# Turning q and k by whole 64-token transposes instead of 64 x 64 products, with loads cut by head

## The chip, the cores and the metric

The kernel runs on one core of one Trainium2 chip. The core has a matrix engine (TensorE, "PE" in the profile, with its weight loads shown apart as "PEld"), a vector engine (DVE), a scalar engine (ACT), GpSimd (POOL) and SyncE (SP), which issues most of the DMAs. The engines run side by side and wait for each other through semaphores. The metric is the device time in microseconds (us) of one execution.

## The reference, cut to what matters

Inputs are q, k and v of shape (8 batches, 8 heads, 576 tokens, 64), a number tau, and the weights of one feed-forward layer.

```python
scores = (1 / 8) * q @ k.T                                # per batch and head, 576 x 576
thresh = scores.max(-1) - tau
attn   = softmax(where(scores >= thresh, scores, -1e9))
x      = (attn @ v) with the heads side by side           # 4608 tokens x 512
h      = x @ w_in                                         # 4608 x 1024
solu   = h * softmax(h)
out    = layernorm(solu) * g_ln @ w_out                   # 4608 x 512, float32
```

## The kernel before

Tokens of a head are split into 512 "main" tokens, laid as 128 partitions times 4 tokens, and 64 "end" tokens. Work on the scores is cut into 144 slots (18 per batch), and the main loop is a loop over rounds, one slot per round. The order of the work on every engine is written out by hand in that loop; no scheduler changes it.

TensorE is used in quarters: nearly all of its products have 64 rows and 64 columns, so that four of them, one per quarter of the array, run side by side. The profile shows this form as `64*64`. A float32 product appears there as two weight loads and two matmuls. In one round TensorE does, in its own order: turns of q and k for a later batch, where some are due (L282); the scores of a slot (L412); one half of the first layer for 128 tokens (`ff_h`, L572) or of the second (`ff_o`, L676); and the product of the attention weights with v for a pair of slots (`attend_steps`, L516). In the last rounds, when no slot is left, the first layer is done by products over the whole array instead (L562, shown as `128*128`).

The scores need q and k with the head dimension on the partitions, so both are turned on TensorE. A pair is two heads of one batch; there are 4 pairs per batch and 32 in all. For a pair, `q_item` and `k_item` turn four blocks (one for each of the 4 tokens of a partition) and `e_item` one block with the end tokens. A block is made by `turn` (L276): for the lower and the upper 64 partitions (r) and the two heads of the pair (y), one 64 x 64 product with a piece of the identity, whose result lands in a spare part of the PSUM tiles that the scores of the round use. So a pair takes 9 calls of `turn`, 36 products. Batch 0 has its own path: its pairs are turned at the start (L767, L822) and by `whole_pair` (L367) in rounds 0, 2 and 4. Pairs of batches 1 to 7 are in the list `preps` (L722), each with the round from which it is due; in a round, as many items as fit into seven spare blocks are turned just ahead of the scores. ACT and DVE copy the turned blocks out (`keep`, L315, L319, L340, L356, L360).

q and k come in by `load_one` (L120), for half a batch (four heads) at a time: one DMA of 512 KB from the SP queue, of 128 partitions x 4 heads x 4 tokens x 64 numbers, so 512 runs of 1 KB. For the first half of a batch it also loads the end tokens of all eight heads (`load_ends`, L138): 64 partitions x 8 heads x 64 numbers, 512 runs of 256 bytes. Rounds for the loads are in `load_at` (L736).

The other DMAs of the SP queue are, in every pair of rounds, four that reorder the transposed attention weights (`blocks`, wT<-T, L491), four that swap halves of a normalised layer (`ff_swap`, V<-u, L654), two stores (L703), and loads of v (L159, L164). SP works through its queue in order. The DMAs are counted on eight semaphores in turn, so each issue also waits until the DMA eight places ahead of it has landed.

## Time and profile before

| | us |
|---|---|
| median of 4 executions | 899.48 (896.93 to 901.35) |
| the profiled execution | 901.35 |
| its span, first to last instruction | 899.4 |
| PE busy | 846.9 (94%) |
| DVE busy | 679.8 (76%) |
| ACT busy | 590.3 (66%) |
| POOL busy | 451.0 (50%) |

A line of a group reads: source line, engine, operation, tiles written and read, form and shape, count; then busy time and the mean duration of one in ns; then the idle time just before, and what ended it. Matmuls overlap, so the mean duration of one is its latency and not the time after which the next can begin; that one is read from starts in the timeline, where a row holds the start, the time from the first start to the last end, and how many instructions are merged.

### The profile page before, as it was taken

Reading aid. Unit: us, or ns where it says so; the run is one execution under the profiler, and the core shown is the slowest. Engines: PE = TensorE matmul, PEld = TensorE weight load, DVE = VectorE, ACT = ScalarE, POOL = GpSimd, SP = SyncE. Lnnn points to the kernel's source line nnn. Section 1 sums busy time; section 2 is a strip of 40 time slices with the busy share of each in tenths; the row PEclk is TensorE's granted clock in tenths of the full one; section 3 lists DMA queues with packets and bytes.
Section 4 is the critical chain, followed back from the end, with each engine's and each line's share of the span. In section 5 each row is a group of like instructions: output and inputs, shape, how many; then the busy total and the mean of one; then the engine's idle time right before and its main releaser. Section 6 shows DMA issues by size and latency. Waiting matters only on the chain. (4 is left out here: it accounts for less than half of the span.)

```text
span 899.4 us, 39683 instructions
## 1 busy us (share of the span) xinstructions
PE 846.9 (94%) x17089; PEld 654.3 (73%) x17089; DVE 679.8 (76%) x1312; ACT 590.3 (66%) x1241; POOL 451.0 (50%) x871
## 2 busy tenths in 40 slices
PE   4668899999999989999999999999999999999997
PEld 3445577878688767777788887878788777777655
DVE  5999886888777757777777877777877877787352
ACT  5867776777777756677766766677767766666121
POOL 2556555555455554555555555555555555555120
PEclk9788899999999999999999999999999999999999
DMA  7999879796867785877886777877887756756322
GB/s 235 247 231 270 215 182 206 176 220 152 216 163 168 165 182 120 187 169 161 192 182 174 179 162 175 187 177 160 186 185 181 180 129 137 171 138 137 78 48 48
DMA packets 95502, 154.61 MB, mean 172 GB/s; under 512 B 27224, under 2 KB 69216, under 8 KB 95328
## 3 DMA queue, kind: packets, MB, share of 16 engines
q1 hardware_dynamic: 94192, 150.09, 71.7%
q8 instruction: 134, 2.20, 1.1%
q10 hardware_dynamic: 1136, 2.00, 0.7%
q14 instruction: 40, 0.33, 0.1%
HBM read 46.14 MB, written 9.44 MB: 62 GB/s over the span
## 5 line engine op out<-in xcount | busy, mean ns | idle before, releaser
L434 DVE CUSTOM_DVE_ANT_0 w<-s_ps,tau_t 128x576 f32<-128x576 f32 x280 | 200.7, 754 | 134.8 <-PE s_ps L412 112.1
L449 ACT ACTIVATE w<-s_ps,nth 128x576 f32<-128x576 f32 x280 | 201.7, 744 | 119.7 <-DVE nth L434 99.2
L676 PE MATMUL o_ps<-w,uT 64*64 64x256 f32 x4608 | 269.7, 376 | 2.0 <-issue 1.0
L676 PEld LDWEIGHTS o_ps<-w,uT 64*64 64x64 f32 x4608 | 234.5, 133 | 44.0 <-issue 10.9
L468 POOL TENSOR_SCALAR w<-w,sm 128x576 f32<-128x576 f32 x288 | 218.1, 769 | 14.3
L572 PE MATMUL h_ps<-w,xh 64*64 64x512 f32 x1856 | 222.1, 591 | 0.9 <-issue 0.9
L458 ACT ACTIVATE w<-w,ntau 128x576 f32<-128x576 f32 x288 | 220.5, 773 | 0.0
L480 DVE STREAM_TRANSPOSE T<-w 128x576 f32<-128x576 f32 x288 | 205.8, 751 | 6.4 <-POOL w L468 6.1
L516 PEld LDWEIGHTS pv<-wT,v 64*64 64x64 f32 x5760 | 171.1, 136 | 38.7 <-issue 22.5
L412 PE MATMUL s_ps<-kT,qT 64*64 64x512 f32 (+1 forms) x2048 | 175.9, 425 | 17.3 <-ACT w L449 16.3
L516 PE MATMUL pv<-wT,v 64*64 64x128 f32 (+1 forms) x5760 | 173.2, 264 | 9.4 <-issue 6.5
L572 PEld LDWEIGHTS h_ps<-w,xh 64*64 64x64 f32 x1856 | 118.0, 134 | 81.3 <-issue 54.1
L465 POOL TENSOR_SCALAR sm<-sm 128x2 f32<-128x2 f32 x144 | 36.4, 253 | 264.8 <-ACT w L458 261.9
L466 POOL TENSOR_TENSOR sm<-sm,mone 128x2 f32<-128x2 f32 x144 | 105.3, 731 | 12.0
L412 PEld LDWEIGHTS s_ps<-kT,qT 64*64 64x64 f32 x2048 | 69.5, 140 | 25.8 <-ACT w L449 21.1
L638 ACT ACTIVATE V<-u,nb,rs 128x1024 f32<-128x1024 f32 x36 | 44.7, 1241 | 52.6 <-POOL nb L628 52.6
L539 ACT COPY xh<-pv 128x256 f32<-128x256 f32 x64 | 23.7, 370 | 62.8 <-PE pv L516 62.8
L587 DVE TENSOR_REDUCE hm<-h_ps 128x1 f32<-128x1024 f32 x36 | 43.1, 1196 | 22.1 <-PE h_ps L572 16.5
L458 ACT ACTIVATION_READ_ACCUMULATOR w<-w,ntau 128x1 f32 x288 | 57.2, 199 | 0.0
L596 ACT ACTIVATE u<-h_ps,hm 128x1024 f32<-128x1024 f32 x36 | 40.3, 1118 | 20.7 <-DVE hm L587 10.3
L602 DVE TENSOR_TENSOR u<-h_ps,u 128x1024 f32<-128x1024 f32 x36 | 42.8, 1190 | 10.4 <-ACT u L596 10.4
L664 DVE STREAM_TRANSPOSE uT<-V 128x1024 f32<-128x1024 f32 x36 | 43.8, 1217 | 9.1 <-DMA V<-u 9.0
(81 smaller groups left out, 632.7 us busy)
## 6 DMA issues: line engine op xcount, KB each, us to landing
wT<-T SPq DMA_DIRECT2D x288, 288.0 KB, 5.7
V<-u SPq DMA_DIRECT2D x144, 64.0 KB, 3.6
out_dram<-ob SPq DMA_DIRECT2D x71, 128.0 KB, 2.8
v<-in_v_dram SPq DMA_DIRECT2D x16, 512.0 KB, 6.3
v<-in_v_dram SPq DMA_DIRECT2D x32, 256.0 KB, 5.8
q<-in_q_dram SPq DMA_DIRECT2D x15, 512.0 KB, 6.2
k<-in_k_dram SPq DMA_DIRECT2D x15, 512.0 KB, 5.7
raw<-in_moe_w_out_dram SPq DMA_DIRECT2D x8, 512.0 KB, 7.5
```

The lines of the kernel that those rows point to most:

```text
L412: nc.tensor.matmul(out=ps[h][ROWS[y], ks], lhsT=lhsT, rhs=d["kT"][ROWS[h], ks], start=True, stop=True,)
L434: nc.vector.tensor_tensor_reduce(out=w, in0=ps[:, 0:S], in1=(zero if loose else tau_t).to_broadcast([P, S]), scale=1.0, scalar=BIG, op0=AL ...
L449: nc.scalar.activation(out=d["w"][x], in_=d["w"][x] if d["loose"] else d["ps"][x][:, 0:S], func=AF.Prelu, bias=d["nth"][x], scale=-1.0, al ...
L458: nc.scalar.activation(out=w, in_=w, func=AF.Exp, bias=ntau, scale=1.0, accum_out=sm[:, x : x + 1])
L466: nc.gpsimd.tensor_tensor(out=sm, in0=sm, in1=mone, op=ALU.pow)
L468: nc.gpsimd.tensor_scalar(out=w, in0=w, scalar1=sm[:, x : x + 1], scalar2=1.0, op0=ALU.mult, op1=ALU.mult)
L480: nc.vector.transpose(out=T[:, :, r, h, :], in_=w)
L516: nc.tensor.matmul(out=to, lhsT=d["v"][ROWS[u], h0 + h, m ^ 4 * u if m < 8 else m], rhs=rhs, start=m == 0, stop=m == NK - 1,)
L572: mm = nc.tensor.matmul(out=h[ROWS[y], f], lhsT=x[ROWS[r], c, ROWS[y]], rhs=w1_parts[ROWS[r], c, part ^ r], start=part == 0 and c == 0, st ...
L638: nc.scalar.activation(out=V, in_=u, func=AF.Identity, bias=nb, scale=rs)
L664: nc.vector.transpose(out=uT, in_=d["V"].rearrange("p y (m x) -> p m y x", x=32))
L676: nc.tensor.matmul(out=d["o"][ROWS[z], 512 * r : 512 * r + 256], lhsT=d["uT"][ROWS[r], m].rearrange("p y x -> p (y x)"), rhs=w2[ROWS[r], m ...
```

## The change

For batches 1 to 7 a block is turned by two transposes of 64 partitions x 128 numbers (64 tokens of both heads of the pair at once), where it was turned by four 64 x 64 products. The two heads of a pair must then lie side by side in one row of the loaded tile. So the tile is laid out as (head pair, token, 2 x 64), and `load_one` fills it by four DMAs, one per head, each of 128 partitions x 4 tokens in runs of 256 bytes. The end tokens already lie side by side. Batch 0 is turned and loaded as before. On PE the order of the items is the same as before, with half as many products in each turn; on SP each q or k load of batches 1 to 7 stands as four DMAs in the place of one; the order on DVE, ACT and POOL is unchanged.

```diff
@@ load_one
+        if b > 0:
+            d[nm] = loads.tile([P, 2, 4, 2 * D], F32, tag=nm, name=nm)
+            for x in range(4):
+                nc.sync.dma_start(
+                    out=d[nm][:, x // 2, :, D * (x % 2) : D * (x % 2) + D],
+                    in_=src[b, 4 * hf + x, 0:SM, :].rearrange("(p t) d -> p t d", t=4),
+                )
+            if hf == 0:
+                if b not in ends:
+                    ends[b] = loads.tile([P, H, D], F32, tag="ends", name="ends")
+                load_ends(b, nm, slice(0, H), nc.sync)
+            return
         d[nm] = loads.tile([P, 4, 4, D], F32, tag=nm, name=nm)
@@ turn
-    def turn(spare, x, lhsT_of):
+    def turn(spare, x, of, whole):
         o = spare["base"] + 64 * x
         to = slice(o, o + 64)
         for r in range(2):
+            if whole:
+                nc.tensor.transpose(
+                    out=spare[r][:, to], in_=of[ROWS[r]], identity=ident[ROWS[r], ROWS[r]]
+                )
+                continue
             for y in range(2):
                 nc.tensor.matmul(
-                    out=spare[r][ROWS[y], to], lhsT=lhsT_of(r, y), rhs=ident[ROWS[r], ROWS[r]],
-                    start=True, stop=True,
-                )
+                    out=spare[r][ROWS[y], to], lhsT=of[ROWS[r], y],
+                    rhs=ident[ROWS[r], ROWS[r]], start=True, stop=True,
+                )
+
+    def tokens_of(i, nm, t):
+        src, h0 = source(i)
+        if i < NP:
+            return src[nm][:, h0 : h0 + 2, t]
+        return src[nm][:, h0 // 2, t]
@@ q_item (k_item the same with "k"), e_item
-                turn(spare, x + t, lambda r, y: src["q"][ROWS[r], h0 + y, ts.start + t])
+                turn(spare, x + t, tokens_of(i, "q", ts.start + t), i >= NP)
...
-            turn(spare, x, lambda r, y: ends[i // NP][ROWS[r], 2 * (i % NP) + y])
+            two = ends[i // NP][:, 2 * (i % NP) : 2 * (i % NP) + 2]
+            turn(spare, x, two.rearrange("p y d -> p (y d)") if i >= NP else two, i >= NP)
```

## The prediction

> **What bounds the kernel now.** First the page: PE 94% busy, and in its row of 40 slices nine tenths or more from the sixth on, but for one. Then the windows by stage.

> ```profile
> span 899.4 us, 39683 instructions
> PE 846.9 (94%) x17089; PEld 654.3 (73%) x17089; DVE 679.8 (76%) x1312; ACT 590.3 (66%) x1241; POOL 451.0 (50%) x871
> ...
> 400.00:500.00 100.00, 100.00 (x2106) 81.41 (x2102) 78.18 (x151) 69.43 (x146) 54.13 (x105) 1.00 0.77 179
> 500.00:600.00 100.00, 98.77 (x2114) 82.42 (x2110) 77.65 (x152) 69.44 (x147) 53.18 (x108) 1.00 0.75 172
> ```

> After the span come PE, PEld, DVE, ACT, POOL, the granted clock and the DMA share. From about 100 us on PE is the bound, at full clock; DVE has a fifth of its time free, the DMA engines a quarter. Busy time alone can hide slack, so I read starts in PE's timeline.

> ```profile
> 505.95 0.28 PE L282 MATMUL s_ps<-ident,k 64*64 64x64 f32 x4
> ...
> 506.65 0.22 PE L412 MATMUL s_ps<-kT,qT 64*64 64x64 f32 x1
> ...
> 507.62 3.77 PE L572 MATMUL h_ps<-w,xh 64*64 64x512 f32 x32
> 511.06 2.19 PE L516 MATMUL pv<-wT,v 64*64 64x128 f32 x70
> 513.02 0.22 PE L412 MATMUL s_ps<-kT,qe 64*64 64x64 f32 x1
> ```

> The 32 passes of L572 take 3.44 us from start to start of what follows: four quarters side by side, no hole. The 24 products of a turn block (48 passes) take 505.95 to 506.65, 0.70 us, 29 ns a product. So a microsecond added to PE here lengthens the run by nearly one, and one saved shortens it.

> **What goes.** 28 pairs x 9 turns x 4 = 1008 products (L282 on s_ps: 896 + 896 + 224 rows, two passes each). At 29 to 31 ns, as the blocks after 200 us show them, 30.2 us.

> **What comes.** 28 x 9 x 2 = 504 transposes. The trace has one transpose, of the gains:

> ```profile
> L190 PE MATMUL g_ps<-ident,g_rows 8*128 8x8 f32 x1 | 0.2, 222 | 1.2 <-ACT qe L356 1.2
> L190 PEld LDWEIGHTS g_ps<-ident,g_rows 8*128 8x128 f32 x1 | 0.1, 133 | 2.5 <-ACT qe L356 2.5
> L562 PEld LDWEIGHTS h_ps<-w,xh 128*128 128x128 f32 x48 | 8.8, 190 | 11.1 <-issue 10.3 <-DVE T L480 0.8
> L282 PEld LDWEIGHTS s_ps<-ident,k 64*64 64x64 f32 x896 | 24.8, 137 | 5.6 <-ACT w L449 4.2 <-DVE both L434 0.5 <-issue 0.3
> ```

> It is one pass, not two, and its load of 128 columns takes 133 ns, like a product's load of 64 columns (median 135) and not like one of 128 (190). In L282's rows a quarter starts a new pass every 60 ns, with that 64-column load hidden behind the pass before. I take 60 ns for a transpose in one half of the array; the two halves (r = 0, 1) hold different rows and run side by side, as the quarters do: 30 ns each, 504 x 30 = 15.1 us. Bounds: 15 ns, a pass's share now (7.6 us); and, if the halves take turns, 60 ns (30.2 us). In series without any overlap, 222 ns each, it would be 112 us; no row here runs so. I stay at 30, since the load's duration is the nearest row.

> [...]

> **Changes of form.** Today turns, scores, layers and pv are all `64*64` and join without a hole. The transposes are 64 rows x 128 columns. They stand in 49 separate blocks on PE (21 of 10 transposes, 14 of 8, 7 of 14, 7 of 12), so PE goes into another form and back 49 times. The trace shows such changes at the end, into `128*128`:

> ```profile
> 823.43 3.70 PE L562 MATMUL h_ps<-w,xh 128*128 128x512 f32 x8
> 827.06 2.20 PE L516 MATMUL pv<-wT,v 64*64 64x128 f32 x72
> 829.18 3.70 PE L562 MATMUL h_ps<-w,xh 128*128 128x512 f32 x8
> 832.82 0.89 PE L516 MATMUL pv<-wT,v 64*64 64x128 f32 x24
> ```

> The same half layer takes 823.43 to 827.06, 3.63, where L572 took 3.44: 0.19 more. The pv block takes 2.12 (827.06 to 829.18) where 511.06 to 513.02 was 1.96: 0.16 more. Together 0.35 us for one change there and back: PE waits about 0.09 each time until the array is empty, and the first weight load is not hidden. With a first load as short as 64 columns it is 0.30; with quarters that end less evenly before a turn, 0.35. I take 0.33: 49 x 0.33 = 16.2 us. Bounds: 0, if only a change of the row split empties the array (the rows stay halved here), and 0.5 (24.5 us).

> [...]

> PE waits ahead of some blocks anyway (idle before L282 on s_ps: 3.5 + 6.3 + 0.5 us, on ACT and DVE); entries there are free: -1.5 us.

> **Loads.** Each of the 28 loads of q or k becomes four DMAs: 84 more on SP, the same bytes.

> ```profile
> L129 SPq DMA_DIRECT2D q<-in_q_dram x17: 392/600/1716, 0.7 to 681.8; - x17
> L140 SPq DMA_DIRECT2D ends<-in_q_dram x9: 612/690/2230, 1.2 to 631.9; - x9
> SPq L491 <- DVE T L480: 196.6, 51, 11.4
> PEld pv L516 <- DMA wT<-T: 1.8, 4, 0.9
> ```

> An issue with 512 runs of 256 bytes takes 0.69 us (the end tokens do it today), so a load takes SP 2.8 us instead of 0.6, about 60 us in all. Queued behind are the wT, V and store DMAs. SP has the time: it waits 196.6 us for the transposed T just ahead of the wT issues that mostly follow a load, and wT lands a median 4 us ahead of its pv (landings against PE's starts). Behind a load SP's wait is 0.1 to 7 us; after 425, 539 and 631 us it is only 0.1, but there wT lands 3 to 6 us early. In the stage of 60 to 110 us four loads meet waits of 1.3, 1.2, 4.1 and 1.0 us and wT is hardly early; I charge 1 us. Between 0, if all is covered, and 28 x 2.2 = 62 us, if nothing were. The packets: 256-byte ones took a mean 21.9 ns in the trace's packet records, 1 KB ones 64.8, so 28 x 512 x (4 x 21.9 - 64.8) = 327 us over 16 engines, 20 us each, 2.3 points of DMA share above 0.75. Hidden behind PE; without that cover it shows in the wT waits above. Where q or k itself is concerned: loads are due 3 to 6 rounds (over 18 us) ahead of their turn, so nothing waits for their later landing.

> The copies on ACT and DVE, their order and their sizes stay: 0.

> **Sum.** -30.2 + 15.1 + 16.2 - 1.5 + 1 = +0.6 us on the profiled execution of 901.35 (span 899.4, 1.95 around it), so 902.0. That execution stands 1.9 above the median 899.48; on the median's scale 900.1. I say 900.

> **Rivals.** [...] (2) No emptying between two forms with the same row split: -16 us, 884. For: the trace shows only changes of rows and columns together. (3) Transposes at a pass's share of 15 ns: -7.5, 892. (4) SP: ten of the 28 loads push a wT 0.8 us past its pv: +8, 908. For: a fifth of the wT land under 1.5 us ahead. Against: those mostly do not follow a load. (5) The change does what it says but PE was not the limit: then nothing but the loads' cost is seen, 900 to 902; the block starts above speak against it.

> **How the numbers follow.** My forecast 0.40 (its own range 893 to 907, from 0.25 to 0.45 us a change of form), (1) 0.20, (2) 0.15, (4) 0.13, (3) 0.08, others, slower, 0.04. Half a per cent (4.5 us) is about what can be told from no change. Faster: (2) mostly, (3), a little of the forecast, 0.25. Slower: (1), (4), the forecast's upper part and the rest, 0.43. Same: 0.32. Range: 887 leaves out most of (2), 917 holds (1) with a longer change; about 2 in 10 outside.

> [...]

## The result, and the profile after

The changed kernel takes 902.76 us (median of 53 executions, 898.06 to 910.05), the kernel before 899.58 (79 executions): a ratio of 1.0043, 95% interval 1.0031 to 1.0055, so 3.9 us slower. The forecast was 900.0, in a range of 887 to 917. The two profiled executions do not show the difference: they took 901.30 and 901.35 us.

The page of the changed kernel, first its span and busy times, then the DMA queues with packets, MB and share of the 16 engines' time:

```profile
span 899.2 us, 36750 instructions
PE 847.5 (94%) x15577; PEld 527.0 (59%) x15577; DVE 679.4 (76%) x1312; ACT 590.9 (66%) x1241; POOL 451.0 (50%) x871
...
q1 hardware_dynamic: 138544, 150.10, 74.0%
q8 instruction: 122, 2.00, 1.0%
```

PE has 1512 records fewer in each column and the same busy time. The DMA share of q1 was 71.7% before; it rose by the 2.3 points that the prediction worked out.

The groups of the transposes, by form, and PE's timeline at the same work as in the prediction (there, 24 products from 505.95 to 506.65):

```profile
L294 PE MATMUL s_ps<-ident,k 64*128 64x64 f32 x224 | 15.4, 238 | 3.6 <-ACT w L470 2.9 <-DVE both L455 0.7
L294 PEld LDWEIGHTS s_ps<-ident,k 64*128 64x128 f32 x224 | 10.5, 140 | 14.3 <-ACT w L479 6.2 <-ACT w L470 4.1 <-issue 2.0
```

```profile
500.32 3.63 PE L697 MATMUL o_ps<-w,uT 64*64 64x256 f32 x64
503.77 1.16 PE L433 MATMUL s_ps<-kT,qT 64*64 64x64 f32 x16
504.75 3.63 PE L697 MATMUL o_ps<-w,uT 64*64 64x256 f32 x64
508.31 0.28 PE L294 MATMUL s_ps<-ident,k 64*128 64x64 f32 x2
508.42 0.23 PE L294 MATMUL s_ps<-ident,ends 64*128 64x64 f32 x2
508.49 0.41 PE L294 MATMUL s_ps<-ident,q 64*128 64x64 f32 x8
508.83 1.21 PE L433 MATMUL s_ps<-kT,qT 64*64 64x64 f32 x16
509.86 3.61 PE L593 MATMUL h_ps<-w,xh 64*64 64x512 f32 x32
```

The form is `64*128`, one row a transpose, loads of 140 ns. The half layer ahead of the block takes 504.75 to 508.31, 3.56 us, where the same one without a block behind it takes 3.45 (500.32 to 503.77): 0.11 for the way into the other form. The 12 transposes take 0.52. The scores behind them take 1.03, where they take 0.98 elsewhere: 0.05. Together 0.68 us, against 0.70 for the 24 products before. So where PE is the bound, turning costs what it did.

What is lost has to be looked for at another place. In the list of waits of the changed kernel, two lines stand out; the columns are the sum in us, the number and the longest:

```profile
PE pv L537 <- DMA wT<-T: 4.6, 4, 2.2
PE o_ps L697 <- DMA w<-w: 2.8, 1, 2.8
```

The first was shorter in the kernel before:

```profile
PE pv L516 <- DMA wT<-T: 1.5, 3, 0.7
```

It is no mark of the loads, though: with the turns alone changed, whose run follows below, it is 4.0 us. The second is new: the kernel before has no wait of PE for `w<-w`. These are the copies that swap the halves of the second layer's weights (`weight_d`, L269 before, L281 after), done once, while batch 1 is loaded. The first use of that layer in PE's timeline, before and after:

```profile
111.19 3.68 PE L676 MATMUL o_ps<-w,uT 64*64 64x256 f32 x62
...
115.62 3.68 PE L676 MATMUL o_ps<-w,uT 64*64 64x256 f32 x62
```

```profile
111.62 3.69 PE L697 MATMUL o_ps<-w,uT 64*64 64x256 f32 x64 [0.30 <-DVE uT L685]
...
116.08 3.22 PE L697 MATMUL o_ps<-w,uT 64*64 64x256 f32 x52
122.12 1.08 PE L697 MATMUL o_ps<-w,uT 64*64 64x256 f32 x12 [2.83 <-DMA w<-w]
```

Before, both blocks run through (the rows of 62 leave out two passes that are interleaved with other work). After, in the second one, PE stands 2.83 us with 12 of 64 passes left, until the last copy lands. SP's timeline shows why it lands late (start, time, how many issues):

```profile
104.07 0.58 SPq L129 DMA_DIRECT2D q<-in_q_dram  x1
...
106.83 3.85 SPq L491 DMA_DIRECT2D wT<-T  x4
110.72 2.16 SPq L269 DMA_DIRECT2D w<-w  x2
```

```profile
63.41 2.71 SPq L127 DMA_DIRECT2D k<-in_k_dram  x4
...
78.53 2.67 SPq L127 DMA_DIRECT2D q<-in_q_dram  x4
...
93.18 2.97 SPq L127 DMA_DIRECT2D k<-in_k_dram  x4
...
108.76 2.65 SPq L127 DMA_DIRECT2D q<-in_q_dram  x4
111.45 1.27 SPq L281 DMA_DIRECT2D w<-w  x2
112.83 3.84 SPq L512 DMA_DIRECT2D wT<-T  x4
116.72 2.25 SPq L281 DMA_DIRECT2D w<-w  x2
```

The last two copies are issued from 110.72 before and from 116.72 after: the four loads of batch 1, each 2.7 to 3.0 us on SP instead of 0.4 to 0.6, stand ahead of them, and SP has almost no gap there. The DMA engines have little room either, as the windows of 60 to 116 us show, the kernel before first (the last three columns are the granted clock, the DMA share and GB/s):

```profile
60.00:116.00 56.00, 44.58 (x804) 30.04 (x800) 51.72 (x100) 39.53 (x87) 30.43 (x46) 0.88 0.96 240
```

```profile
60.00:116.00 56.00, 43.51 (x686) 26.71 (x682) 49.66 (x94) 37.84 (x85) 29.52 (x45) 0.88 0.95 211
```

The share is nearly full in both, and with the loads in 256-byte packets the stage moves 211 GB/s where 240 went before. From these four loads alone, 8192 packets of about 22 ns in place of 2048 of about 59, each of the 16 DMA engines gets 3.7 us more work in a stage where its share is 0.95 and more.

### The profile page after: what moved, and what is told of

It is laid out like the page before. It is cut to its first block, busy times and chain, and to the rows that moved or that the text cites. A ratio compares the mean times of both kernels' runs of the same rounds, so it can differ in the third digit from the quotient of the medians.

```text
span 899.2 us, 36750 instructions
## 1 busy us (share of the span) xinstructions
PE 847.5 (94%) x15577; PEld 527.0 (59%) x15577; DVE 679.4 (76%) x1312; ACT 590.9 (66%) x1241; POOL 451.0 (50%) x871
## 5 line engine op out<-in xcount | busy, mean ns | idle before, releaser
L697 PE MATMUL o_ps<-w,uT 64*64 64x256 f32 x4608 | 263.5, 376 | 4.1 <-DMA w<-w 2.8
L697 PEld LDWEIGHTS o_ps<-w,uT 64*64 64x64 f32 x4608 | 188.2, 133 | 93.4 <-issue 22.0
L593 PE MATMUL h_ps<-w,xh 64*64 64x512 f32 x1856 | 215.2, 592 | 2.6 <-issue 2.6
L537 PEld LDWEIGHTS pv<-wT,v 64*64 64x64 f32 x5760 | 157.4, 137 | 51.0 <-issue 38.1
L433 PE MATMUL s_ps<-kT,qT 64*64 64x64 f32 (+1 forms) x2048 | 166.1, 429 | 13.5 <-ACT w L470 12.4
L537 PE MATMUL pv<-wT,v 64*64 64x128 f32 (+1 forms) x5760 | 164.9, 264 | 9.1 <-DMA wT<-T 4.6
L593 PEld LDWEIGHTS h_ps<-w,xh 64*64 64x64 f32 x1856 | 76.0, 134 | 125.0 <-issue 113.3
L433 PEld LDWEIGHTS s_ps<-kT,qT 64*64 64x64 f32 x2048 | 54.8, 138 | 28.9 <-ACT w L470 17.8
L617 ACT ACTIVATE u<-h_ps,hm 128x1024 f32<-128x1024 f32 x36 | 40.2, 1117 | 21.9 <-DVE hm L608 14.6
```

The lines of the kernel that those rows point to most:

```text
L433: nc.tensor.matmul(out=ps[h][ROWS[y], ks], lhsT=lhsT, rhs=d["kT"][ROWS[h], ks], start=True, stop=True,)
L537: nc.tensor.matmul(out=to, lhsT=d["v"][ROWS[u], h0 + h, m ^ 4 * u if m < 8 else m], rhs=rhs, start=m == 0, stop=m == NK - 1,)
L593: mm = nc.tensor.matmul(out=h[ROWS[y], f], lhsT=x[ROWS[r], c, ROWS[y]], rhs=w1_parts[ROWS[r], c, part ^ r], start=part == 0 and c == 0, st ...
L697: nc.tensor.matmul(out=d["o"][ROWS[z], 512 * r : 512 * r + 256], lhsT=d["uT"][ROWS[r], m].rearrange("p y x -> p (y x)"), rhs=w2[ROWS[r], m ...
```

## The experiments

All ratios are to the kernel before on the same chip, with 95% intervals.

### The loads or the turns

First the changed kernel again, then each part alone, then a load on the turns.

> The changed kernel once more, on the chip of the next three: 1.004 times the kernel before, as already measured (1.0043), so about +4 us. It is the mark against which the two halves of the change are read.

Measured: 905.98 us, 1.0079 (1.0051 to 1.0106). PE waits 3.3 us for `w<-w` in its profile. So the ratio of one and the same kernel differs by 0.4% between two measurements; a difference of that size between runs on different chips says little.

The loads alone: turned by products of the tile laid out by pairs.

```diff
-        return src[nm][:, h0 // 2, t]
+        return src[nm][:, h0 // 2, t].rearrange("p (y d) -> p y d", y=2)
-                turn(spare, x + t, tokens_of(i, "q", ts.start + t), i >= NP)
+                turn(spare, x + t, tokens_of(i, "q", ts.start + t), False)
...                                              # k_item and e_item alike
```

> Loads of q and k by four DMAs of single heads, turns by products as before. Theory P (what is paid lies on PE, in the 49 changes of form): 0 to +1 us. Theory L (the changes of form are paid for by the shorter blocks, and what is left over comes from 84 more issues on SP and 43,000 more packets): +3 to +5 us, with the waits of pv and of the layers for DMAs as large as in the changed kernel, some 5 us and more.

Measured: 901.35 us, 1.0038 (1.0015 to 1.0060); a wait of 4.0 us for `w<-w`.

The turns alone: whole loads as before, the transposes take 128 neighbouring numbers of the tile.

```diff
-        if b > 0:
-            ...                                    # the four DMAs by head
-        return src[nm][:, h0 // 2, t]
+        at = D * (4 * h0 + t)
+        return src[nm].rearrange("p h t d -> p (h t d)")[:, at : at + 2 * D]
```

> Turns by transposes, q and k loaded by one DMA as before. Part of the computation is changed: a transpose takes 128 numbers side by side of the loaded row, which here are two neighbouring tokens of one head and not the two heads of one token, so the scores of batches 1 to 7 are of other numbers; every size, order and wait is that of the changed kernel. Theory P: +3 to +5 us. Theory L: -1 to +1 us. If both parts cost, 1 to 3 us here.

Measured: 898.84 us, 1.0003 (0.9979 to 1.0027). Nothing waits for `w<-w`; in its PE timeline the block runs through:

```profile
113.98 3.63 PE L686 MATMUL o_ps<-w,uT 64*64 64x256 f32 x64
117.55 0.47 PE L282 MATMUL s_ps<-ident,k 64*128 64x64 f32 x8
```

This and the changed kernel have the same work in the same order on PE; they differ in the loads alone, by 0.4% (by 0.76% with the repeated run, on the same chip). So the loads cost 3.5 to 7 us and the turns between -2 and +2.4.

Each transpose issued three times:

```diff
-                nc.tensor.transpose(out=spare[r][:, to], ...)
+                for _ in range(3):
+                    nc.tensor.transpose(out=spare[r][:, to], ...)
```

> The changed kernel with every transpose issued three times in a row, so 1008 more in the same 49 blocks. At 30 ns each, two halves side by side (the forecast): +30 us against the changed kernel. At 60 ns (halves in turn): +60. At 15 ns: +15. The copies of one block follow each other in the same half here, so if the load of a half can't overlap its own pass, it shows as up to 80 us.

Measured: 925.05 us, 1.0293 (1.0251 to 1.0335), 19 us more than the changed kernel on the same chip and 22 more than its median. In its PE timeline, 42 transposes stand where 14 did:

```profile
506.71 0.97 PE L295 MATMUL s_ps<-ident,q 64*128 64x64 f32 x24
507.51 0.73 PE L295 MATMUL s_ps<-ident,k 64*128 64x64 f32 x18
508.17 1.21 PE L434 MATMUL s_ps<-kT,qT 64*64 64x64 f32 x16
```

24 of them take 0.80 us, 33 ns each, and a block of 42 takes 0.565 us longer than one of 24, 31.4 ns for each one more. So the 31 to 32 ns a transpose (62 to 63 between two starts in one half of the array) holds for long blocks too. The 1008 more are 32 us of PE time, of which the run grew by about two thirds; where the rest went is told below, in the section on the prediction.

### More issues or smaller packets, and at which batch

The kernel before with its loads of batches 1 to 7 in four DMAs of 1 KB runs:

```diff
-            queue.dma_start(out=d[nm][:, part]..., in_=src[b, hs, 0:SM, :][part]...)
+            for h in [slice(i, i + 1) for i in range(4)] if b > 0 else [part]:
+                queue.dma_start(out=d[nm][:, h]..., in_=src[b, hs, 0:SM, :][h]...)
```

> Kernel before with each q and k load of batches 1 to 7 issued as four DMAs of one head, still in runs of 1 KB: 84 more issues on SP, no more data packets. Theory I (SP's issue time is what the loads cost): +3 to +4 us, most of it between 60 and 116 us of the span, where SP has no free time; the wT issues there come 3 to 6 us later. Theory D (the 256-byte packets crowd the DMA engines): 0 to +0.5 us.

Measured: 895.19 us, 0.9962 (0.9932 to 0.9993). More issues alone cost nothing, and that although PE waits for `w<-w` here too:

```profile
119.37 0.93 PE L677 MATMUL o_ps<-w,uT 64*64 64x256 f32 x10 [2.64 <-DMA w<-w]
```

The kernel before with two DMAs a load, in runs of 256 bytes:

```diff
+        if b > 0:
+            to = d[nm].rearrange("p h t d -> p (h t) d").rearrange("p (n x) d -> p x n d", x=2)
+            of = src[b, hs].rearrange("h s d -> (h s d)")[0 : P * 16 * D]
+            of = of.rearrange("(x p n d) -> x p n d", x=2, p=P, d=D)
+            for x in range(2):
+                nc.sync.dma_start(out=to[:, x], in_=of[x])
+            ...                                    # the end tokens as before
```

> Kernel before with each q and k load of batches 1 to 7 as two DMAs of 1024 runs of 256 bytes: the packets of the changed kernel with 28 more issues, not 84. Part of the computation is changed: the numbers loaded are of the right size and count, but lie in another order, so the scores of batches 1 to 7 are of other numbers. Theory I: +1 us if an issue costs the same however many runs it has, and up to +3 if its time goes with the runs. Theory D: +3 to +4 us.

Measured: 903.82 us, 1.0060 (1.0026 to 1.0094), with a wait of 2.6 us for `w<-w`. The smaller packets cost, not the number of issues: batch 1's loads take SP 1.3 to 2.1 us each here, and 1.8 to 2.8 us in the run before this one, which lost nothing. (The two loads of batch 1's end tokens, just behind them, take 2.5 and 4.0 us here and 0.6 and 0.7 us there.)

The changed kernel with batch 1 loaded and turned as before (three more conditions changed alike):

```diff
-        if b > 0:
+        if b > 1:
-        if i < NP:
+        if i < 2 * NP:
```

> The changed kernel with batch 1 loaded and turned as before, batches 2 to 7 as changed. Theory S (the loads cost where SP and the DMA engines are full, in the first 116 us, and nothing later): -2 to 0 us against the kernel before, since the blocks on PE are shorter and nothing is paid. If the cost is spread over all 28 loads: +2 to +4 us.

Measured: 893.49 us, 0.9933 (0.9909 to 0.9957). No wait for `w<-w`.

The kernel before with only batch 1's four loads cut by head (products as before):

```diff
+        if b == 1:
+            ...                                    # the four DMAs by head
```

> Kernel before with only the four q and k loads of batch 1 cut into four DMAs of 256-byte runs, turns by products. Theory S: +2 to +4 us, all between 60 and 116 us. If the cost is spread over all 28 loads: 0 to +0.6 us.

Measured: 906.58 us, 1.0082 (1.0053 to 1.0110). In its PE timeline:

```profile
115.75 3.22 PE L697 MATMUL o_ps<-w,uT 64*64 64x256 f32 x52
123.29 1.55 PE L697 MATMUL o_ps<-w,uT 64*64 64x256 f32 x10 [4.32 <-DMA w<-w]
```

and its windows around the stop (the number behind POOL's count is the granted clock):

```profile
120.90:124.30 3.40, 1.01 (x12) 0.65 (x16) 0.00 (x0) 1.24 (x1) 2.43 (x5) 0.50 0.77 213
124.30:127.70 3.40, 3.40 (x66) 2.56 (x62) 0.00 (x0) 0.58 (x1) 0.00 (x0) 0.50 1.14 236
127.70:131.10 3.40, 3.19 (x138) 3.02 (x133) 2.96 (x10) 1.37 (x5) 0.00 (x0) 0.99 0.98 227
```

Four loads of 28 are enough for the whole loss. PE stops after the same 52 passes, for 4.32 us, and works at half its clock until 127.7.

### The same again, and a kernel that is faster than both

> The changed kernel with batch 1 loaded and turned as before, once more: 0.993 times the kernel before (-6 us), as measured the first time. If that was chance: 0.996 to 1.000.

Measured, the kernel of 0.9933 once more: 893.36 us, 0.9945 (0.9925 to 0.9965).

Products throughout, loads cut by head from batch 2 on (`if b > 1`, `turn(..., False)`):

> Kernel before with the q and k loads of batches 2 to 7 cut into four DMAs of 256-byte runs, those of batch 1 whole, turns by products. Tells what the gain of the version above is made of. If it is the shorter blocks on PE: 0 to +1 us here. If it comes from cutting the loads (as the run with four 1 KB issues a load suggests): -3 to -5 us here.

Measured: 899.98 us, 1.0010 (0.9979 to 1.0041). The other 24 loads cost nothing that can be told from zero, so the place of the loads decides.

The kernel from batch 2 on, with batch 1's loads as four DMAs of 1 KB runs (both edits above):

> The version from batch 2 on, with batch 1's q and k loads issued as four DMAs of one head in runs of 1 KB, turned by products. If four issues of 1 KB help by themselves in the full stage: another -1 to -3 us, 0.990 to 0.992. If that gain belonged to the later batches: 0.993, the same as without it.

Measured: 892.02 us, 0.9923 (0.9893 to 0.9953), not to be told from the one without that edit. PE waits for `w<-w` in its trace as well:

```profile
119.56 1.07 PE L698 MATMUL o_ps<-w,uT 64*64 64x256 f32 x10 [2.85 <-DMA w<-w]
```

So this wait alone is not the loss: two kernels have it and lose nothing. When does the loss arise? The starts of the 65th transpose `T<-w` on DVE, the same work in every kernel, tell it. It starts at 200.1 us in the trace of the kernel before, at 197.4 to 200.3 us in the five others with batch 1's loads whole (mean of all six 198.9), at 199.1 and 199.6 us in the two with four 1 KB DMAs, and at 200.2 to 205.3 us in the five with 256-byte runs (mean 202.8). The means are 3.9 us apart, where the medians gave 3.5 to 7 us for the loads. So the loss arises in the first 200 us, while batch 1 is loaded and soon after. How much of it is the wait for the last copy, and how much arises ahead of it, these traces do not tell.

These two kernels, from batch 2 on and with batch 1 in four, beat the kernel before by 5 to 7 us and the changed one by 9 or more. By the blocks on PE, though, turning batches 2 to 7 saves nothing, and the turns alone gave 1.0003. PE's stops that no semaphore explains led to the last run: the same kernel with 64 transposes of the identity at the very start.

```diff
         first = dict(enumerate(tiles), base=0)
+        for _ in range(32):
+            for r in range(2):
+                nc.tensor.transpose(
+                    out=tiles[r][:, 0:64], in_=ident[ROWS[r]], identity=ident[ROWS[r], ROWS[r]]
+                )
```

> The kernel that keeps batch 1 as it was and turns batches 2 to 7 by transposes (0.9933 and 0.9945 of the kernel before), with 64 transposes of the identity (128 PE instructions with their weight loads) at the very start, where PE has nothing to do from 1.4 us until the first k lands at 5.6 us. So nothing is added to the path; every later PE instruction stands 128 places further on in PE's program. Theory A (PE's stops without a semaphore belong to the supply of its program in pieces of 256 instructions): the stops stay at places 193 beyond a multiple of 256, and so stand at other work than in the kernel without the 64, and the time may move by several us either way (0.990 to 1.002). Theory B (the stops belong to the work, or the gain has nothing to do with them): the stops stay at the same work, now 65 beyond a multiple of 256, and the time is as without the 64, 0.992 to 0.996 of the kernel before.

Measured: 900.82 us, 1.0027 (1.0007 to 1.0046). PE's timeline without the 64, then with them:

```profile
5.60 1.13 PE L299 MATMUL tp<-ident,k 64*64 64x64 f32 x32 [5.60 <-DMA k<-in_k_dram]
...
448.69 2.17 PE L697 MATMUL o_ps<-w,uT 64*64 64x256 f32 x36 [1.62 <-issue]
```

```profile
1.37 3.68 PE L790 MATMUL tp<-ident 64*128 64x64 f32 x64 [1.37 <-POOL ident masks.py:199]
5.58 1.13 PE L299 MATMUL tp<-ident,k 64*64 64x64 f32 x32 [0.52 <-DMA k<-in_k_dram]
...
244.30 1.30 PE L697 MATMUL o_ps<-w,uT 64*64 64x256 f32 x18 [0.94 <-issue]
...
537.99 0.65 PE L433 MATMUL s_ps<-kT,qT 64*64 64x512 f32 x3 [0.98 <-issue]
```

The 64 are over before the first k lands at 5.58, as it did at 5.60, and the first maximum on DVE starts at 10.3 us in place of 10.4: nothing is added to the path. Yet the median is 7 us longer, and the intervals lie apart. The stops have moved to other work. Counted in PE's recorded instructions (matmuls, weight loads and semaphore instructions), all stops after 200 us of at least 0.25 us without a semaphore stand here:

| kernel | counts at the stops | us each |
|---|---|---|
| before | 7617, 8129, 12225, 20929, 29633 | 0.46, 0.61, 3.80, 1.23, 0.91 |
| changed | 7105, 10945, 15041 | 1.67, 0.52, 2.56 |
| turns alone | 10945, 15041, 18881 | 2.02, 2.54, 1.25 |
| from batch 2 | 15809, 27073 | 1.62, 1.01 |
| from batch 2, 64 places on | 8129, 19393, 23489 | 0.94, 0.98, 0.26 |

Every one is 193 past a multiple of 256, and so are the 33 in the other nine traces. So they belong to the place in PE's program and not to the work (theory A). That these stops are what makes the 7 us is argued, not shown: the profiled execution of the last kernel was the fastest of its twelve (896.28 us), with stops of 2.2 us in all, and no trace of a slower one is there. The granted clock, on record for every execution, points the same way: its mean is 0.971 over the twelve of the last kernel, and 0.977 over the 22 without the 64 as well as for the kernel before on the last one's chip. By an estimate, 0.006 of 900 us is 5.4 us of full clock, most of the 7. One rival is untested: the last kernel ran on another chip than the two runs without the 64, which were not repeated there. The step from 0.9933 and 0.9945 to 1.0027 is twice the 0.4% by which the changed kernel's own ratio differed. So the gain of 0.6% from batch 2 on can't be put down to the turning: with the same work, moved to another place in PE's program, it was gone.

## Why the prediction was right or wrong

**What goes.** Right: 24 products in 0.70 us before, about 30 us in all.

**What comes.** Right: 31 to 32 ns a transpose where 30 was forecast (two more in a block make it 63 ns longer). The halves run side by side: a transpose started every 31 to 32 ns, with a load latency of 140. So the bound of 60 ns, for halves that take turns, falls, and with it what the chances count as (1). Rival (3), 15 ns, falls too.

**Changes of form.** Right, a little high. From the end of the last pass ahead of it to the first score, a block of 8, 10, 12 or 14 transposes takes 0.49, 0.55, 0.61 or 0.67 us where no wait falls into it, so the 49 take 27.3 us; the slower scores behind them, 49 x 0.05, make it 29.8. Without 504 transposes of 31.5 ns that leaves 0.28 a change there and back, in place of 0.33. In 45 of the 49 entries the first transpose starts 200, 306 or 520 ns after the start of the last pass, which has 128, 256 or 512 columns: 107 ns for every 128 columns, and 93 ns more each time. (The other four stand behind longer waits.) The rows stay halved, so rival (2) falls: with a change of columns alone these 93 ns are there. That they are the time until the array is empty, as the prediction has it, was its author's estimate; no trace shows what PE does in them. Against 30.2 before, PE's side is about zero (forecast with the entries behind waits: -0.4). The turns alone, at 1.0003, say the same.

**A microsecond on PE is a microsecond of the run.** True where PE does not wait, by the run with three transposes for one. Its lag behind the changed kernel, read from the starts of the transposes `T<-w` in the two profiles, grows by 13.4 us between 462 and 778 us, where the added transposes are 13.8 us of PE time. Over the whole run 32 us more on PE gave 19 to 22 us. The profiles, 25 us apart, put what is missing in two places. By 228 us the lag is 5.4 us for 8.6 us of added transposes, since in the first batches PE has waits for other engines (busy for 70.0 of the 90 us from 45 to 135 in the changed kernel), and added work goes into them. And at 442 us the changed kernel has a stop of 2.56 us with a halved clock behind it (0.5 from 445.4 to 448.8 us), which the other one does not have; there the lag falls by 4.5 us.

**Loads.** This is the term that was mis-sized: "I charge 1 us" for the stage of 60 to 110 us. With the same work on PE, the loads cost 3.5 to 7 us, and batch 1's alone gave 1.0082. The stage was the right one, and a load took SP 2.7 to 3.0 us, where 2.8 was forecast. But the wait that is new there is not one for a wT of the main loop, as rival (4) had it. It is the one for the last copy of the second layer's weights, issued 6 us later, with PE waiting 2.6 to 4.3 us in the five traces with 256-byte loads of batch 1 and, in three of them, a halved clock after it (0.50 in the windows shown above). That this wait is the whole of the cost is not shown: with four 1 KB DMAs a load PE waited 2.6 and 2.9 us at the same place, and nothing was lost. I looked behind the loads for wT alone, and I took the packets' 20 us a DMA engine at the share of the whole run, 0.75, where this stage has 0.96. For batches 2 to 7 the step held: 1.0010 with their loads cut, and SP's wait for T fell from 196.6 us to:

```profile
SPq L512 <- DVE T L501: 128.9, 39, 8.6
```

That is 68 us shorter, near the 60 us that the prediction reckoned for the longer loads on SP, and pv's waits for wT stayed at a few us (4.6, from 1.5).

**The sum.** 900.0 was forecast, 902.76 measured; the 3 us are of the size of what the term of the loads was short by, and the terms on PE came out as forecast. But the last run moved by 7 us with the same work, at another place in PE's program and on another chip. No term of the sum had that in it, and the forecast cannot be called exact to less.

## What to carry to other kernels

Cost a transfer's extra packets and issues in the stage where they run, by that stage's own DMA share and by everything that is queued behind them there, one-time copies too. A change of layout that is free in the steady state can be left out for the one stage where it isn't; here that is the first batch loaded beside the weights (1.0082 with its loads alone cut by head, 1.0010 with those of the other six). A difference of under 1% between kernels whose instruction counts differ on the bounding engine needs a control that shifts the program without changing the work, before it is put down to the work.

## What the runs showed of the hardware that was not expected

```profile
336.04 0.58 PE L516 MATMUL pv<-wT,v 64*64 64x64 f32 x9 [3.80 <-issue]
...
338.02 1.75 PE L412 MATMUL s_ps<-kT,qT 64*64 64x64 f32 x16
339.51 2.85 PE L676 MATMUL o_ps<-w,uT 64*64 64x256 f32 x48
```

```profile
335.60:339.00 3.40, 2.96 (x30) 1.79 (x34) 0.53 (x1) 0.37 (x1) 0.00 (x0) 0.51 1.03 224
```

The 16 passes of L412 take 1.49 us here (338.02 to 339.51) and 0.97 elsewhere.

Left open: why four issues of 1 KB runs alone gave 0.9962, and why the costs do not add up: batch 1's loads alone gave 1.0082 and all loads 1.0038, with the same work on PE, though on different chips. How full the DMA engines are at the places of the stops could be a reason for both; it was not tried.
